# A polynomial-sketch attention and feed-forward kernel on one core: sketch loads on another queue, a new order of all steps, a last store in two halves

## The chip, the cores and the metric

The kernel runs on one core of one Trainium2 chip. The metric is the device time of one execution in microseconds, as the median of several runs. The engines are named as in the profile: PE is TensorE's matmul, PEld its loading of weights, DVE is VectorE, ACT is ScalarE, POOL is GpSimd, and SP is SyncE, whose queue issues most transfers.

## The reference

Two blocks follow each other. The first is an attention whose scores are a product of two sketches; `S1` and `S2` are 8 x 32 in float64, and q, k, v are 4 batches x 4 heads x 1088 positions x 32 in float32:

```python
def phi(x):                                   # 64 features of each position
    a = einsum('rd,bhsd->bhsr', S1, x)
    b = einsum('rd,bhsd->bhsr', S2, x)
    return einsum('bhsi,bhsj->bhsij', a, b).reshape(..., 64)
q_p, k_p = phi(q), phi(k)
kv = einsum('bhsf,bhsd->bhfd', k_p, v)        # summed over positions
z = k_p.sum(axis=2)
x = (q_p @ kv) / (q_p . z + 1e-06)            # then heads side by side: 4352 x 128
```

The second is a multiplicative feed-forward block with float64 weights, `((x @ w1) * (x @ w2)) @ w3 @ w_out`, with 128 model and 1024 inner columns. The result is 4352 x 128 in float32. The denominator can come close to zero, so the kernel splits operands into a leading part and a rest and multiplies these apart.

## The kernel before

The kernel is a set of 952 named steps. Each step is a small function that issues one or a few instructions. The text `ORDER` (lines 61 to 115) lists the names, the steps are issued in that order, and lines 1526 to 1534 chain the instructions of each engine, so that every engine works through its own steps strictly in the listed order. Nothing is reordered later: an instruction that waits holds up all that its engine has behind it. `POOL` and `ACTS` (lines 52 to 58) name the steps that run on GpSimd and ScalarE; other vector steps run on VectorE (`on`, line 148). `SLOTS` (lines 28 to 44) gives each new tile its buffer by hand; the kind `b` is the eight PSUM banks.

The names say what a step works on. `s.` is the preparation of the sketches: `s.load` loads S1 and S2 (line 252), `s.words` to `s.rest` turn float64 words into float32 parts, `s.T`, `s.R` and `s.blk` spread them over the partitions. `k0` to `k3` are the keys of the four batches. Of them `load` and `loadr` fetch the main part (8 x 128 positions a head) and the remaining 64 positions, `max`, `g`, `lead` and `rest` find a scale and split the keys (lines 566 to 596; `rest` is one subtraction on line 596), `gram0` to `gram4` multiply the split keys with themselves (line 604), `Gm` to `Nr` make the denominators' operand out of that, `kp` makes the 64 features (line 622), `kv` and `kvr` sum them with the values (lines 714 and 721). `kr0` and `kr1` handle the remaining keys of two batches at once (`kr0.kp`, line 785, on GpSimd). `q0` to `q4`, `q6` and `qr` are the queries in groups; their steps run from `tr` and `max` through products `A0`, `C0`, `C1` (lines 964 to 1298), splits `sm`, `st`, `sh`, `sl`, `sc`, the sum `al`, the products `p01`, `p2`, `p12`, the denominator `dn`, `de`, `rc`, the features `phi` and the result `x`, which `xT` copies as the operand of the feed-forward block. `w0` to `w10` load and convert the weights (the last sum on GpSimd, lines 442 and 445), and `f0` to `f7` multiply w3 by w_out (line 478).

The feed-forward block works on eight groups of 512 rows, `g0` to `g7`, and one of 256, `gr`. Each has eight chunks; `g0.3a` and `g0.3b` are the two products of chunk 3 (lines 1448 and 1458), `g0.3c` copies the first out of PSUM on ScalarE, `g0.3m` multiplies them on VectorE (line 1464), and `g0.3o` adds the product into the output (line 1471). These 128 x 512 products are the main matmuls. A group ends with `oT` and `st`, four stores on the sync queue. The last group `gr` has two row halves, with products `o0` and `o1` (line 1478), copies `oT0` (ScalarE) and `oT1` (VectorE), and stores `st0` (ScalarE's queue) and `st1` (sync queue), 64 KB each (line 1432).

72 idle matmuls on a tile of zeros (`warm0` to `warm28`, line 221, in groups of 16, 10, 6, 4, 2 and 1) are steps like the others.

In the order before, the sync queue starts with `s.load`, `k0.loadr`, `q0.load`, `k1.loadr`, `k1.load`, and ScalarE's queue with `k0.load0`, `k0.load1`. The gram of the fourth batch comes right behind the `kv` of the third on TensorE:

```python
"... kr1.kp q4.sc q4.al k2.kv0 k2.kv3 k2.kv1 k2.kv2 k3.ab k2.kvr k3.gram0 k3.gram1 k3.gram2 k3.gram3 k3.gram4 ..."
```

Of the kernel before, what the change touches and what calls it, by code (L numbers as in the profile page):

```python
# [66 lines left out]
k1.lead0 k1.tr1 warm23 q0.A0 warm15 w1.load kr0.ab warm4 warm12 kr0.abc k1.rest0 q1.l2 warm13 warm7 warm18 q0.C0 k0.N0
kr0.kp w1.m v0.load q0.sma q0.C0t q0.sta k0.N1 k0.kv0 k0.kv3 k1.gram0 k1.gram1 k0.kv1 q1.l1 k0.kv2 kr1.load v0.loadr
k0.kvr s.RC k0.Na warm10 warm21 kr1.tr k0.kvc k0.kvm q0.sha q0.sla k0.Nb k2.zero k0.Nh w0.load warm17 k1.tr0 kr1.kT
q0.sca k1.kT1 k1.kT0 k0.kzt q1.A0 k0.kz q0.A1 kr1.ab q0.al q0.phi0 q0.phi1 q1.sm q0.smy q0.sty q1.st q0.pt0 warm5  # L70
k0.kqt k0.Nl warm20 k0.Nf w0.m kr1.abc q0.pc0 q0.pt1 q0.shy q1.rm q0.C1 k1.gram2 k1.gram3 k1.gram4 q0.pc1 warm19 q0.x0
q1.load k0.Nr q0.sly q0.C1t q0.x1 w0.c q0.scy q0.p01 q0.p2 q1.sh q0.p12 q0.dn s.KS w0.j q1.C0 q0.de q1.sl q0.rc q0.xs
q0.xt q0.xT k1.ab w0.a1 v1.zero k2.load k2.loadr k2.max w1.c warm24 w0.a0 warm22 g0.3a q1.sca q1.p01 g0.3c k2.g
v1.loadr k1.Gm k2.lead0 q1.scy q1.al w2.load q1.p2 q1.p12 k1.abt q1.restT q1.dn g0.1a g0.3b w1.j q1.de k0.kq q1.rc
k1.Gt g0.3m q1.bs g0.2b w1.a0 q1.phi g0.0a g0.5a g0.4a q1.pt0 g0.0c w2.c g0.1c w3.load w2.m k2.rest0 q1.pt1 g0.6a
g0.2a q1.pc0 w2.j k1.Ga k1.kp0 q1.pc1 g0.5c g0.2c g0.6c k2.gram0 q2.tr k1.Gb k1.T0 k2.gram1 k1.T1 q2.max k1.Ta k1.Tb
k1.Ts w2.a0 w4.load q1.x w1.a1 k2.gram2 k2.gram3 k2.gram4 k1.N0 k1.N1 s.AR warm16 k2.Gm q1.xT g1.7a q2.l2 k2.Gt k2.Ga
g0.6b g0.0b w3.c q2.l1 k1.Na k1.Nb k1.Nr k2.Gb w4.m g0.4c g0.6m g0.1b g0.7a g0.0m q2.rm w4.c q2.C0 q2.A0 q2.C1 g0.1m
w4.j w3.j g1.7c warm28 g0.7c w3.m g1.4a g1.2a g0.7b q3.tr q2.Ct g0.2m g1.6a q2.At g1.6c w4.a0 w3.a0 g1.1a g1.7b
q2.load q3.max q4.tr w6.load v1.load w2.a1 w4.a1 g1.2c f1.t g0.7m w3.a1 g1.1c w6.c q3.l2 g1.5a g1.7m q3.l1 q2.sm f0.t  # L80
g1.3a g0.4b f1.m w9.load warm27 f0.m q2.st q2.sh q4.max f0.o q2.sl g1.5c g0.4m q2.sc f1.o g1.3c g1.2b q2.p01 q3.rm
v2.zero k1.kp1 q2.al q2.p2 q2.p12 g1.2m k1.kv0 k2.T0 k1.kv2 k1.kv3 k2.T1 k1.kv1 k1.kvr q3.C0 q3.A0 q3.C1 w5.load
k1.kvc g1.4c k1.kqt k2.Ta k2.Tb q2.dn k2.Ts q2.de w6.j q2.rc g1.0a q3.Ct q2.bs g1.3b g1.6b g1.5b g1.3m q2.phi0 q3.At
w6.m g0.5b w5.m w5.c g1.5m g1.1b g1.0b g1.6m q3.sm g0.0o w9.c k1.kq w9.m g0.1o g1.0c k2.N0 k2.N1 q2.pT0 g0.5m q2.x0
g1.0m q3.st g1.1m q2.restT warm11 k3.zero w6.a0 k2.Na q3.sh w7.load kh2.load w6.a1 q3.sl w9.j k2.Nr w5.j q2.xT0 g1.4b
w9.a0 w9.a1 w5.a0 f3.t g1.0o q3.load g2.6a w10.load k3.loadr g2.6b g1.1o g2.1a g2.6c q4.l2 q4.l1 w7.m g2.1c w7.c g2.6m
g1.4m k2.Nb f6.t f3.m q3.sc g2.3a g2.7a g2.7c f3.o g2.3c q3.p01 q3.al k2.kT1 w5.a1 q3.p2 q3.p12 q3.dn k2.kT0 q4.rm
f6.m f6.o w10.c w8.load k2.ab w8.c q4.C0 q4.A0 q4.C1 w7.j k2.abt warm9 g2.4a f2.t q4.Ct g1.6o g2.0a f2.m g2.2b k3.load
q4.At q4.sm q3.de w7.a0 g2.0c f2.o v2.loadr w7.a1 kh3.load g0.2o f4.t q3.rc w10.m f4.m g2.2a k2.kp0 g0.6o f4.o q3.bs
w8.m w8.j g1.3o w8.a0 v2.load q3.phi0 g2.2c g2.4c w10.j q3.pT0 q3.x0 w8.a1 g0.3o q3.xT0 g2.7b w10.a0 w10.a1 k2.kp1  # L90
f5.t k3.max q6.tr f5.m g3.0b k3.kT1 g2.7m q3.restT f7.t g3.0a f5.o g3.0c g3.0m g3.3a g0.5o g3.3c g2.1b g2.2m g3.4a
g1.4o g1.5o k3.kT0 q6.max k3.g g2.1m g3.4c g2.5b f7.m f7.o g1.2o g2.0b q4.st q4.sh k3.lead0 q4.sl g3.7a g1.7o g3.7c
k3.rest0 kr1.kp q4.sc q4.al k2.kv0 k2.kv3 k2.kv1 k2.kv2 k3.ab k2.kvr k3.gram0 k3.gram1 k3.gram2 k3.gram3 k3.gram4
k2.kvc q4.p01 k2.kqt q4.p2 g2.0m k3.abt k3.Gm g0.4o g2.5a q4.p12 g2.5c k2.kq q4.dn q4.de k3.Gt g2.5m g3.6b g2.4b g2.0o
g3.6a q4.rc g3.6c k3.Ga q4.bs g1.oT g2.4m q4.phi0 q4.phi1 q4.pT0 k3.Gb g0.7o g3.4b g3.4m v3.zero k3.kp0 v3.load
v3.loadr g3.3b g2.4o g2.3b g2.3m g3.6m q4.pT1 g0.oT qr.max g3.2a g3.1a g2.6o g2.5o g3.2b g2.3o g3.3m k3.kp1 g3.1c
g3.2c qr.l2 k3.T0 k3.T1 k3.Ta g3.2m q4.x0 q4.x1 k3.kv0 k3.kv1 k3.Tb k3.N0 k3.kv3 k3.kv2 k3.kvr k3.Ts q6.l2 q6.l1 k3.N1
q6.rm k3.Na q4.xT0 warm6 k3.Nr k3.Nb q4.xT1 g4.2a g2.2o g5.2a g4.2c q6.C0 q6.A0 k3.kvc q6.C1 g5.2c q6.At q6.Ct q6.sm
k3.kqt g2.1o g4.3a g3.0o g5.4a g4.0a g2.7o g5.3a q6.st g4.0c g5.4c g5.3c g4.3c q6.sh q6.sl g5.0a q6.sc q6.p01 q6.al
q6.p2 q6.p12 g5.3b g2.oT g5.3m q6.dn g5.4b g5.7a q6.de k3.kq q6.rc qr.l1 qr.rm q6.bs q6.phi0 q6.phi1 g5.4m g5.1a  # L100
q6.pT0 g3.1b g5.1c g3.5a g5.7b g3.5c g5.0c g5.7c g3.1m q6.pT1 g3.4o g3.5b g3.3o q6.x0 q6.x1 q6.xT1 q6.xT0 g5.1b g5.7m
g5.1m g3.5m g5.0b g6.6a g3.7b g5.0m g3.7m qr.C0 g6.6c qr.A0 qr.C1 qr.At warm25 g6.0b g6.0a g6.0c g6.0m qr.Ct qr.sm
g5.2b g7.4a g4.1a g6.5a g4.4a g4.4c g4.1c qr.st qr.sh qr.sl g3.1o g5.2m g7.2a g3.6o g3.2o g4.5a g3.5o g4.5c g7.2c
g7.0a g4.4b g5.0o g5.1o g5.5a g5.2o g7.0c g7.4c g5.5c g6.2a qr.sc g4.4m qr.al g7.6a g6.4a g6.2c g6.5c g6.4c g5.6a
qr.p01 g5.6c g7.5a g6.7a g7.6b g7.5c g5.4o g6.2b g7.6c g7.0b g5.6b g5.5b g6.7c g6.2m g4.0b g7.4b g5.3o g5.5m g5.6m
g7.5b g6.4b g7.4m g5.5o qr.p2 g7.6m g6.1a g5.6o g3.7o g4.2b qr.p12 g4.0m g7.0m g7.5m g6.7b qr.dn g4.6b g6.5b g6.7m
g3.oT g6.5m g7.2b qr.de g4.6a g4.6c g7.2m g4.6m g6.6b g5.7o g7.3a g6.3a g4.7a g6.4m g4.2m g6.6m g5.oT g7.7b g6.1b
g7.7a g7.3c g7.7c g7.7m qr.rc g7.3b qr.bs g5.st g7.1b g6.3c g7.0o g7.1a g7.1c g7.6o g6.1c g6.3b g7.5o g4.0o g4.7c
g7.4o g6.3m g7.3m g7.1m qr.phi0 g7.2o qr.pT0 qr.x0 g4.4o qr.xT0 g4.5b gr.7a gr.7c gr.1a g7.3o g6.1m gr.1c g4.5m g3.st
g0.st g7.1o g7.7o g4.1b g4.1m gr.4a gr.7b gr.1b gr.3b gr.0b gr.3a gr.4c gr.3c gr.7m g7.oT gr.3m gr.1m g4.7b gr.2a  # L110
# [1454 lines left out]
```

## Time and profile before

| | |
|---|---|
| median of 3 runs | 254.58 us (254.56 to 255.01) |
| the profiled execution | 254.37 us, its span 252.6 us |
| granted TensorE clock | 1.00 throughout |
| busy: PE, DVE, ACT, POOL | 246.1, 160.0, 99.7, 66.8 us |
| first main matmul (a_ps, line 1448) | 30.29 us |
| last matmul ends | 249.41 us |
| from HBM, to HBM | 19.40 MB, 2.23 MB |

The span runs from the first to the last instruction; the profiled execution's own time is 1.77 us longer. TensorE's matmuls are pipelined, so the starts of successive ones are what shows a pause. VectorE is busy for 0.92 to 0.98 of nearly every 6 us between 6 and 36 us, and less and less after 90 us; GpSimd is busy for 15.4 us of the first 30.3, and for 1.1 us behind 200. Transfers take place before 90 us for the most part; the stores follow after 200.

### The profile page before, as it was taken

What the parts mean: (1) busy time and instruction counts of PE and PEld (TensorE: products, weight loads), DVE (VectorE), ACT (ScalarE), POOL (GpSimd) and SP (SyncE); (2) the same over time, 40 slices, a digit from 0 to 9 for tenths busy, and PEclk for the clock granted to TensorE, in tenths of its full rate; (3) what the DMA queues carried; (4) which work ended last, traced back from release to release, by engine and by line L of the source; (5) the groups of instructions that cost most, each with busy time, mean ns of one, the idle gap of its engine ahead of it and who ended that gap; (6) DMA issues with size and microseconds to landing.
All of it is one profiled execution on the core that took longest, in us unless ns stands there. A gap on an engine that the chain in (4) does not pass through costs nothing.

```text
span 252.6 us, 5980 instructions
## 1 busy us (share of the span) xinstructions
PE 246.1 (97%) x2503; PEld 137.9 (55%) x2503; DVE 160.0 (63%) x358; ACT 99.7 (39%) x183; POOL 66.8 (26%) x99
## 2 busy tenths in 40 slices
PE   8799999999999999998999999999999999999994
PEld 6689845457456576456446444444444444456554
DVE  2999998989998995938677597550115371424040
ACT  4588398763918543340225143213340012211010
POOL 4644535393546309203540016010000001000000
PEclk9999999999999999999999999999999999999999
DMA  6867793996679930200000000000000007205014
GB/s 182 262 173 263 222 241 84 259 254 139 160 206 235 249 90 0 85 6 3 3 0 3 3 0 1 4 0 0 3 0 0 0 2 123 44 0 83 0 28 76
DMA packets 31130, 22.01 MB, mean 87 GB/s; under 512 B 21248, under 2 KB 25600, under 8 KB 30976
## 3 DMA queue, kind: packets, MB, share of 16 engines
q1 hardware_dynamic: 30416, 21.05, 33.9%
q10 hardware_dynamic: 688, 0.59, 0.7%
q8 instruction: 19, 0.31, 0.5%
q14 instruction: 7, 0.06, 0.1%
HBM read 19.40 MB, written 2.23 MB: 86 GB/s over the span
## 4 chain that ended last, share of the span: by engine, by line
PE 95%; issue 1%; DMA 1%; POOL 1%; ACT 1%; DVE 0%; SPq 0%; POOLq 0%; ACTq 0%
PE a_ps L1448 23%; PE b_ps L1458 23%; PE ps_o L1471 22%; PE ps_w3o L478 6%; PE ps_g L604 3%; PE ps_x L1408 2%; PE idle_ps L221 2%; PE ps_ac L1294 2%; PE ps_kv L714 2%; PE ps_or L1478 1%; DMA s_raw<-in_S_dram 1%; PE ps_ab L672 1%; PE ps_ab L647 1%; PE ps_xt L1195 1%; PE ps_kt L630 1%
## 5 line engine op out<-in xcount | busy, mean ns | idle before, releaser
L1464 DVE TENSOR_TENSOR ab<-ffa,b_ps 128x512 f32<-128x512 f32 (+1 forms) x72 | 44.9, 649 | 60.8 <-PE b_ps L1458 40.9
L1453 ACT COPY ffa<-a_ps 128x512 f32<-128x512 f32 (+1 forms) x72 | 38.6, 566 | 96.4 <-PE a_ps L1448 93.8
L1448 PE MATMUL a_ps<-xT,w 128*128 128x512 f32 (+1 forms) x144 | 66.7, 570 | 0.0
L1458 PE MATMUL b_ps<-xT,w 128*128 128x512 f32 (+1 forms) x144 | 65.5, 569 | 0.0
L1471 PE MATMUL ps_o<-ab,w3o 128*128 128x512 f32 x128 | 62.3, 594 | 0.0
L1448 PEld LDWEIGHTS a_ps<-xT,w 128*128 128x128 f32 x144 | 26.5, 190 | 30.0 <-issue 23.9
L1458 PEld LDWEIGHTS b_ps<-xT,w 128*128 128x128 f32 x144 | 26.9, 190 | 29.1 <-issue 25.0
L1471 PEld LDWEIGHTS ps_o<-ab,w3o 128*128 128x128 f32 x128 | 23.9, 190 | 25.5 <-issue 24.0
L442 POOL TENSOR_TENSOR w3c<-cv_c,cv_m 128x512 int32<-128x512 int32 x16 | 20.8, 1333 | 22.0 <-DVE cv_c L431 13.7
L1389 POOL TENSOR_TENSOR ph<-s_al,s_bs 128x1024 f32<-128x1024 f32 (+1 forms) x6 | 10.8, 1808 | 52.7 <-DVE s_bs L1379 52.7
L478 PEld LDWEIGHTS ps_w3o<-wo,w3T 128*128 128x128 f32 x128 | 15.4, 192 | 3.6 <-issue 3.3
L478 PE MATMUL ps_w3o<-wo,w3T 128*128 128x128 f32 x128 | 15.6, 275 | 0.0
L221 PE MATMUL idle_ps<-zeros 128*128 128x256 bf16 x72 | 13.3, 317 | 1.0 <-DVE zeros L193 1.0
L229 ACT ACTIVATE cv_c<-raw 128x1024 f32<-128x1024 f32 x11 | 12.8, 1175 | 2.1 <-DMA raw<-in_moe_w_dram 2.1
L417 ACT ACTIVATE cv_m<-raw 128x1024 int32<-128x1024 uint32 x11 | 12.8, 1178 | 0.0
L472 DVE STREAM_TRANSPOSE w3T<-w3c 128x1024 f32<-128x1024 f32 x8 | 9.8, 1230 | 3.5 <-POOL w3c L442 3.5
L604 PE MATMUL ps_g<-kk 128*32 128x64 f32 x288 | 8.2, 225 | 2.1 <-POOL kk L596 1.1
L1346 POOL TENSOR_TENSOR s_al<-s_hl 128x128 f32<-128x128 f32 (+2 forms) x3 | 2.3, 753 | 29.7 <-DVE s_hl L1341 29.7
L1419 ACT COPY xT<-ps_x 128x128 f32<-128x128 f32 (+2 forms) x20 | 4.6, 325 | 13.1 <-PE ps_x L1408 9.5
L1397 DVE STREAM_TRANSPOSE pT<-ph 128x1024 f32<-128x1024 f32 (+1 forms) x7 | 8.2, 1164 | 2.5 <-POOL ph L1389 2.4
L221 PEld LDWEIGHTS <-zeros 128*128 128x128 bf16 x72 | 7.5, 114 | 3.9 <-issue 1.0
L604 PEld LDWEIGHTS ps_g<-kk 128*32 128x32 f32 x288 | 7.0, 109 | 2.8 <-POOL kk L596 1.2
(241 smaller groups left out, 284.3 us busy)
## 6 DMA issues: line engine op xcount, KB each, us to landing
raw<-in_moe_w_dram SPq DMA_DIRECT2D x32, 256.0 KB, 7.6
qh<-in_q_dram SPq DMA_DIRECT2D x4, 544.0 KB, 3.5
out_dram<-oT SPq DMA_DIRECT2D x33, 64.0 KB, 2.0
raw<-in_moe_w_dram SPq DMA_DIRECT2D x4, 512.0 KB, 5.8
k<-in_k_dram SPq DMA_DIRECT2D x3, 512.0 KB, 5.9
v<-in_v_dram SPq DMA_DIRECT2D x2, 512.0 KB, 6.4
raw<-in_moe_w_out_dram SPq DMA_DIRECT2D x1, 1024.0 KB, 6.0
kh<-in_k_dram SPq DMA_DIRECT2D x8, 128.0 KB, 6.3
```

What stands on the lines that cost most here:

```text
L221: pe.matmul(t, zeros, bview(zeros, [[0, 2], [1, 128]]), start=True, stop=True)
L229: act.activation(dst, hi.bitcast(F32), ACT.Prelu, scale=2.0 ** -112, alpha=-2.0 ** 32)
L417: act.mul(x["m"], words(0).bitcast(U32), 2.0 ** -29)
L442: pool.tensor_tensor(d, c, m, ALU.add)
L478: pe.matmul(t["o"], w3T[ko][:, c], wo[:, c], start=c == 0, stop=c == NC - 1)
L604: pe.matmul(o[h * D:(h + 1) * D], lhs, rhs, start=start, stop=stop, skip_group_check=True)
L1389: on(nm(f"phi{u}")).tensor_mul(x, bview(s["al"][:, u * g], [[r, g], [1, r], [0, r]]), bview(s["bs"][:, u * g], [[r, g], [0, r], [1, r]]))
L1448: pe.matmul(x["a"][:, :w], w_of(0, c), xT[g][:, c0:c0 + w], start=True, stop=True)
L1453: act.copy(x["s"][:, :w], x["a"][:, :w])
L1458: pe.matmul(x["b"][:, :w], w_of(1, c), xT[g][:, c0:c0 + w], start=True, stop=True)
L1464: dve.tensor_mul(ab_sb[g, c][:, c0:c0 + w], x["s"][:, :w], x["b"][:, :w])
L1471: pe.matmul(o_ps[g], w3o[:, c], ab_sb[g, c], start=c == 0, stop=c == NC - 1)
```

## The change

S1 and S2 are issued on ScalarE's queue in place of the sync queue, and in the new order they stand between `k0.load0` and `k0.load1`. `k0.loadr` and `k1.loadr` are the first two on the sync queue. All 952 steps have a new order, and the buffers (`SLOTS`) are assigned anew. Some steps change their engine. To VectorE from GpSimd go `k0.rest0`, `k1.kp1`, `k2.kp1`, `k3.kp0`, `q0.phi1`, `q1.p2`, `q1.p12`, `q2.al`, `q2.p2`, `q4.p12`, `q6.p12`, `q6.phi0`, `q6.phi1`, `qr.p2`, `qr.phi0`, `s.Pp`, `s.blkh`, `s.rest` and `s.sum`; to GpSimd from VectorE go `k0.Nf`, `k0.Nl`, `k0.kp1`, `k2.kp0`, `k2.rest0`, `k3.kp1`, `k3.rest0`, `q0.al`, `q0.p01`, `q0.phi0`, `q0.scy`, `q1.p01`, `q2.bs`, `q3.p01`, `q3.phi0`, `q4.p01`, `q4.p2`, `q4.sc`, `q6.p01`, `q6.p2`, `qr.bs` and `qr.p01`. `k3.lead0` goes from ScalarE to VectorE. The store `gr.st1` becomes two of 16 tokens x 4 batches each, `gr.st1` on the sync queue and `gr.st2` on ScalarE's. The work and its instructions are otherwise the same.

```diff
@@ the first steps and those around k0.kvr, k3.gram and the end
-s.load k1.zero c.ident c.mask k0.zero c.zeros warm0 k0.loadr k0.load0 k0.load1 c.act s.words s.pair s.lead q0.load
-k0.max0 k0.max1 k0.g k0.lead0 warm1 k1.loadr s.low s.sum s.four k0.tr0 k0.lead1 s.rest s.T k0.kT0 k0.rest0 warm8 q0.tr
...
-gr.5o0 gr.1o0 gr.4o0 gr.0o1 g4.oT gr.6o1 gr.5o1 gr.3o0 g6.oT g4.st g6.st gr.1o1 gr.2o0 gr.7o0 gr.4o1 gr.oT0 gr.3o1
-gr.2o1 gr.7o1 gr.st0 gr.oT1 gr.st1
+k1.zero s.zero c.mask k0.zero k0.loadr c.zeros warm0 warm10 warm11 k1.loadr warm23 warm7 warm22 c.ident q0.load
+k0.load0 k0.max0 s.load k0.load1 k1.load c.act s.words s.pair s.low s.four s.lead k0.tr0 k0.max1 s.sum k0.g k0.lead0
+k0.lead1 s.rest k0.rest0 warm20 warm24 k0.tr1 warm1 s.T k0.gram0 k0.gram1 s.tc k0.rest1 s.R s.P k0.gram2 k0.gram3
...
+s.Pp q0.A0 k0.Tb k0.Ts q0.C0 k0.abc1 w1.m w1.c k0.N0 k0.N1 v0.load k0.kp1 k1.rest0 warm8 k1.tr0 q0.sma kr0.load warm14
+kr0.tr q0.sta q0.C0t q1.max kr0.kT warm4 warm27 warm15 kr0.ab kr0.abc k0.Na q0.sha q0.sla q0.sca k0.Nh kr0.kp q0.al
+kr1.load v0.loadr q1.l2 k1.kT1 q0.phi0 k0.Nb k1.gram0 k1.gram1 k0.kv0 k0.kv3 k0.kv1 k0.kv2 k0.kvr w0.load q0.phi1
...
+f3.m q6.tr q3.restT g1.2m g3.6a q6.max f3.o q6.l2 g3.6c f4.m f4.o k3.lead0 f7.t g3.1b f5.m f7.m g3.5a q6.l1 g3.1c
+k3.rest0 k2.kT1 q4.sh q4.sl g3.5c f7.o k3.kT0 g3.1m q4.sc k3.gram0 k3.gram1 k3.gram2 k3.gram3 k3.gram4 k2.ab k2.abt
...
+gr.0o0 gr.6o0 gr.5o0 gr.1o1 gr.1o0 gr.4o1 gr.3o1 gr.2o1 gr.7o1 gr.4o0 g3.st gr.3o0 gr.2o0 gr.7o0 gr.oT0 gr.oT1 g4.st
+g6.st gr.st1 gr.st2 warm25 gr.st0
...
     @step("s.load")
     def _():
         for i, x in enumerate((S1, S2)):
-            sp.dma_start(s_raw[:, i], x)
+            act.dma_start(s_raw[:, i], x)
...
-    def rest_dst(oT, u):
-        (sp if u else act).dma_start(bass.AP(tensor=out.tensor, offset=(NT - 2 + u) * DM,
-                             ap=[[NT * DM, 32], [S * DM, B], [1, DM]]), oT)
+    def rest_dst(oT, u, t0=0, n=32):
+        (sp if u and not t0 else act).dma_start(bass.AP(tensor=out.tensor, offset=(NT - 2 + u + t0 * NT) * DM,
+                             ap=[[NT * DM, n], [S * DM, B], [1, DM]]), oT[t0 * B:(t0 + n) * B])
...
-                step(f"g{g}.st{u}")(lambda u=u: dst(z[u], u))
+                if u == 0:
+                    step(f"g{g}.st0")(lambda: dst(z[0], 0))
+                else:
+                    for i in range(2):
+                        step(f"g{g}.st{1 + i}")(lambda i=i: dst(z[1], 1, 16 * i, 16))
```

The other edits replace `dve` by `on(...)` in the steps `rm`, `sc`, `p01` and `bs`, so that `POOL` can name them.

More of the change, by code (lines that the diff above doesn't have):

```diff
@@ L52 @@
 POOL = set("""
-    k0.Nh k0.rest0 k0.rest1 k1.kp1 k2.kp1 k3.kp0 q0.phi1 q1.al q1.p12 q1.p2 q2.al q2.p12 q2.p2 q2.phi0
-    q3.p2 q4.al q4.p12 q4.phi0 q4.phi1 q6.p12 q6.phi0 q6.phi1 qr.al qr.p2 qr.phi0 s.Pp s.blk s.blkh
-    s.low s.rest s.sum
+    k0.Nf k0.Nh k0.Nl k0.kp1 k0.rest1 k2.kp0 k2.rest0 k3.kp1 k3.rest0 q0.al q0.p01 q0.phi0 q0.scy q1.al
+    q1.p01 q2.bs q2.p12 q2.phi0 q3.p01 q3.p2 q3.phi0 q4.al q4.p01 q4.p2 q4.phi0 q4.phi1 q4.sc q6.p01
+    q6.p2 qr.al qr.bs qr.p01 s.blk s.low
 """.split())
-ACTS = set("k0.lead1 k1.lead0 k2.lead0 k3.lead0 s.lead".split())
+ACTS = set("k0.lead1 k1.lead0 k2.lead0 s.lead".split())
@@ L67 @@
[L67 to L110, printed above, removed]
-g6.0o gr.5a g1.st gr.2c gr.5c g4.3b gr.2b g4.7m g4.3m gr.5b g4.1o g4.2o g4.5o g4.6o gr.6b g7.st g2.st g4.3o g6.5o
@@ new lines @@
+warm16 w3.load k1.abt k2.g q2.tr g0.5a q2.max k1.Gm q1.restT w1.a1 q3.max g0.4a g0.0a g0.3a g0.7a g0.4c g0.0c g0.2a
+q1.al q1.p01 q1.p2 q1.p12 q1.dn w0.a1 g0.5b g0.3c k2.lead0 g0.5c q1.de k1.Gt s.AR q1.rc g0.3b g0.6a k1.Ga q1.bs g0.0b
+q1.phi g0.2b g0.7c g0.6c q1.pt0 k1.Gb g0.3m k2.rest0 w4.load w5.load g0.0m q1.pt1 k1.kp1 w3.c k1.T0 k1.T1 q1.pc0
+k2.gram0 k2.gram1 k2.gram2 k2.gram3 k2.gram4 k1.Ta k1.Tb k1.Ts w3.m q1.pc1 k2.Gm g0.5m k1.N0 k1.N1 k1.Na q1.x warm18
+k1.Nb q2.l2 q2.l1 g0.2c q1.xT g0.4b q2.rm k1.Nr g0.2m w3.j q2.C0 q2.A0 q2.C1 q2.Ct q2.At w5.m w5.c g1.5b g0.4m q2.sm
@@ new lines @@
+q2.st q2.sh k2.Gt k2.Ga q2.sl w2.load q2.sc q2.p01 w4.c q2.al k1.kp0 w4.j q2.p2 g1.5a g1.6a g1.3a w4.m q2.p12 g1.3c
+g1.6c g0.1a g1.0a w2.m g1.0c g1.3b g1.2a g1.0b g1.5c g0.1c g1.7a w3.a0 w3.a1 g1.3m k2.Gb q2.load v1.load g1.1a g1.7b
+q3.l2 q3.l1 g1.0m q3.rm q2.dn w2.c g1.5m w9.load q2.de w2.j g1.2c g1.1c q2.rc f0.t k1.kv0 k2.T0 k1.kv2 k1.kv3 k1.kv1
+k2.T1 k1.kvr k1.kvc q3.C0 q3.A0 q3.C1 w2.a1 q2.bs k2.Ta g1.7c k2.Tb q3.Ct q3.At g0.1b g1.4a v2.zero q2.phi0 w2.a0
+q3.sm k1.kqt g0.7b g1.6b g1.4b g0.1m g1.7m g0.6b g1.1b q2.pT0 w8.load g1.4c k1.kq g1.4m g1.6m k2.Ts g1.1m k3.zero
@@ new lines @@
+k3.loadr q2.x0 k2.N0 k2.N1 w9.c q3.st w9.j w4.a0 w9.m q2.xT0 w4.a1 q3.sh f1.t q3.sl f0.m g2.4a g2.1a w6.load q3.sc
+k3.load w5.j q4.tr q4.max q3.al q3.p01 f0.o w8.c g2.4c q3.p2 w9.a0 w9.a1 w8.m warm21 w6.c g2.1c g2.1b g2.0a q3.p12
+g0.7m g2.1m f1.m g2.2a g2.6a g2.6c g2.5b g0.6m k2.Na q4.l2 f6.t w8.j g2.0c g2.2c q3.dn f1.o q4.l1 q3.de g2.5a q3.rc
+g2.7a g2.3a g2.7c q3.bs k2.Nr q4.rm k2.Nb f6.m w5.a0 f6.o g2.5c w5.a1 g2.0b f2.t w6.m g2.0m q4.C0 q4.A0 q4.C1 f2.m
+w6.j g2.3c w10.load w7.load q3.phi0 f2.o q4.At warm13 q4.Ct q4.sm q2.restT q3.pT0 w10.c w7.c w10.m g0.0o w7.m g2.6b
@@ new lines @@
+g1.4o g2.3b k2.kp1 g3.6b g2.3m g3.2c f5.o g1.5o k2.kp0 g3.3b g3.3m g3.6m q4.de qr.max q4.rc q4.bs g2.0o g0.5o g2.4o
+g2.6o g2.5o q4.phi0 g2.7m q4.pT0 v2.load v2.loadr q4.phi1 v3.loadr v3.load g1.2o g1.7o g1.oT g3.4a kr1.kp g0.4o g3.2b
+k3.Gt g0.7o qr.l2 g3.4c q4.pT1 k3.Ga k2.kv0 k2.kv3 k2.kv1 k2.kv2 k2.kvr k3.T0 k3.Gb k3.T1 k3.ab k2.kvc k2.kqt k3.Ta
+k3.Tb k3.abt k2.kq g2.3o g3.7b g3.2m q4.x0 q4.x1 k3.Ts k3.N0 k3.N1 q4.xT1 g2.2o q4.xT0 k3.kp0 k3.Na g3.4b k3.Nb k3.Nr
+g0.oT q6.rm g3.4m k3.kp1 k3.kv0 k3.kv1 k3.kv3 k3.kv2 k3.kvr q6.C0 q6.A0 q6.C1 q6.Ct q6.At q6.sm q6.st q6.sh q6.sl
```

65 lines of the change are left out of this document (42 added, 23 removed).

## The prediction

> **What bounds the kernel now.** I read the page first: its busy line and its row of slices say that TensorE never rests.
>
> ```profile
> PE 246.1 (97%) x2503; PEld 137.9 (55%) x2503; DVE 160.0 (63%) x358; ACT 99.7 (39%) x183; POOL 66.8 (26%) x99
> PEclk9999999999999999999999999999999999999999
> ```
>
> A busy matmul row is not proof of work, so the second view is the chain that ended last. It is one TensorE chain from 9.29 us to the end; the only pieces in it that are not matmuls are these:
>
> ```profile
> 1.20 2.50 DMA s_raw<-in_S_dram
> ...
> 6.87 1.05 issue
> 7.96 1.28 POOL kk L596
> 9.29 0.99 PE ps_g L604 x41
> ...
> 117.48 0.99 issue
> ```
>
> The third view is the timeline: the start on VectorE, then the end.
>
> ```profile
> 1.53 0.73 SPq L516 DMA_DIRECT2D k<-in_k_dram  x1
> 5.63 1.41 DVE L180 TENSOR_REDUCE k_m<-k 128x1 f32<-128x576 f32 x2 [0.87 <-DMA k<-in_k_dram]
> ...
> 248.85 0.64 ACTq L1432 DMA_DIRECT2D out_dram<-oT  x1
> 249.45 0.29 DVE L1498 COPY oT<-ps_or 128x128 f32<-128x128 f32 x1 [2.85 <-PE ps_or L1478]
> 249.77 0.62 SPq L1432 DMA_DIRECT2D out_dram<-oT  x1
> ```
>
> So four stretches can change. (1) 0 to 30.29 us, where the first main matmul (g0.3a) starts. The waits of VectorE there list three items, the last of them the 0.87 us for the keys; after 5.63 VectorE never waits, so its queue paces this stretch, and TensorE fills its spare time with idle matmuls (L221). (2) 30.29 to 249.41, where TensorE streams without a pause. (3) Inside it, 1.17 us without a matmul from 117.30 to 118.47. (4) The tail, 249.41 to 252.58. The profiled execution took 254.37 us, a span of 252.6 and 1.77 around it; the median shown is 254.58, so I add 0.21 to what I work out from the trace.
>
> **The first stretch.** The same real TensorE steps stand ahead of the first main matmul in both orders, so everything is in the time at which that matmul starts.
>
> *VectorE's queue.* max0 waits for k0.loadr, issued at 1.53; the view of line 516 has 4.0 to 4.9 us to landing (median 4.1). First on its queue it is issued at about 0.74, where S1 went before, and lands near 4.85, 0.8 us earlier. ScalarE issues S1 and S2 between k0.load0 and k0.load1: two issues of 0.34 (median of line 252) put load1, and the table load behind it, 0.7 later. The table load ended at 3.02, so s.words starts near 4.05 in place of 3.79, still before max0 is over. From max0 to q0.xs VectorE took 5.63 to 28.01, 22.4 us. The new queue takes in s.pair (0.68 from start to next start), s.sum and s.rest (0.43), rest0 (0.6, from k1.rest0's 1.36 for 1152 columns), s.blkh and s.Pp (0.6), phi1 (0.6), w1.j (0.63), and gives away kp0's twin k0.kp1 (1.15), al, phi0, Nl, Nf, scy, p01 (together 1.75) and q1.sl (0.4): +0.2. VectorE alone would start the main stage 0.8 - 0.2 = 0.6 earlier, at 29.7.
>
> *TensorE's queue.* rest0 leaves GpSimd (1.28) for VectorE (0.6), so gram0 can start near 8.85 in place of 9.29. From gram0 to the first main matmul the steps and their idle matmuls sum to 20.9 us (20.99 measured before for a sum of 21.1), plus about 0.3 of waiting for rest1: 30.05.
>
> *GpSimd's chain.* This is the risk. kr0.kp now stands behind k0.Nh, which needs k0.Na. Walking VectorE's queue from 4.85 with the distances above gives the end of Na at 20.15, so kr0.kp starts at 20.4, and k0.kvr on TensorE (20.22 before) waits for it. For kr0.kp the trace has two durations:
>
> ```profile
> L785 POOL TENSOR_TENSOR kpr<-krab x2: 633/1205/1777, 17.4 to 101.9; 128x256 f32<-128x256 f32 x2
> ```
>
> The 1.777 one began at 17.45, just after VectorE's subtraction k1.rest0 (17.38 to 18.74, two SBUF inputs); the 0.633 one at 101.91 met a transpose and a product out of PSUM. So kvr is free at 21.1 to 22.2, and 9.0 us of TensorE steps lie from it to the first main matmul: 30.1 to 31.2, and 31.5 if q0.al and phi0, also on GpSimd now, are waited for. The Trainium skill (SBUF — State Buffer, section Who interferes with whom) states this as a rule: a VectorE instruction with two SBUF inputs and a GpSimd one that reads SBUF exclude each other for a whole instruction. The trace agrees (1.777 - 0.633 = 1.14 us, and 1.2 of k1.rest0 lay ahead), and the rule speaks against every product that this change moves to GpSimd.
>
> Three bounds: 29.7, 30.05, 30.1 to 31.5. I take 30.6, near the middle of the chain's own range since VectorE's steps beside it are short (0.28): **+0.3 us**, ends -0.6 and +1.2.
>
> **Idle matmuls.** 72 in both. Ahead of the first main matmul stood 62, now 66; behind it 10, now 5, since warm25 goes behind the last matmul that counts. In a running stream one takes 0.107 (0.43 for four in the chain): **-0.54**. What lies ahead is already in the 30.6.
>
> **The 1.17 us at 117.3.** No engine released it ("issue"). Instruction queue 8 moved 19 packets and 0.31 MB, 16 KB each; TensorE's 5006 recorded instructions over 19 packets are some 260 per packet. One packet, and no other transfer, moves between 115.5 and 118.6, at about 116.15. From 115.60 to 117.30 TensorE ran 299 instructions: k2.kv, k3.ab, k2.kvr and k3.gram are one run of 464 short ones. My reading: a packet's worth was used up faster than the next arrived, some 2.8 us after TensorE entered the one before (115.67 to 118.47). In the new order k2.kv stands far behind k3.gram; the run is 320 instructions (a weight load and a matmul for each pass, two passes in float32, counted from the steps), and 3072 lie ahead of it, twelve times 256. With some 25 waits counted in, a packet ends inside f7.m, 1.4 us ahead of the run, and the next is needed 232 instructions into it, 1.3 us later: 2.7 us against 2.8. So about 0.1 remains, 0.3 allowed for data traffic: **-0.9**, ends -1.17 and 0. The other runs (k2.gram, k3.kv with q6.C0) have main matmuls between, over 3.3 us per 256 instructions.
>
> **The tail.** The last products are now those of row half 0: oT0 (ScalarE, 0.27), then st2 and st0 issue on ScalarE, in this order. st2's data is ready 0.9 us earlier, so it can issue while the copy runs; its length, a half of 64 rows, lies between 0.33 (line 909's shortest) and 0.64. st0 then starts 0.45 to 0.7 after the last matmul instead of 0.36, and is still the whole 64 KB. st1 and st2 save nothing, being earlier anyway: **+0.1**, ends 0 and +0.35. Were there no st2 ahead, the copy alone would decide and the term be zero.
>
> **The middle.** VectorE's queue is lighter by 1 to 4 us over most of the stream (sums of its steps at equal TensorE work), GpSimd's heavier by up to 8 at 90 us and 5 at the end. TensorE paused nowhere there but at 117.3, so nothing is left to gain; a loss can come from any step that now ends late. **+0.2**, ends 0 and +1.5.
>
> **Sum:** 0.3 - 0.54 - 0.9 + 0.1 + 0.2 = -0.84. 254.37 - 0.84 = 253.5, with the 0.21 **253.7 us**. About 0.2% (0.5 us) is what a measurement of this kernel can tell from no change.
>
> **Rivals.**
> *GpSimd paces the first stretch fully:* first main matmul at 31.5, so +1.2 in place of +0.3: the sum is +0.06, **254.6**, the same. For it: VectorE's next step phi1 waits for GpSimd's al. Against it: long two-input products are rare there. Chance 0.17.
> *Slower, GpSimd holds k3.gram0:* k3.rest0 goes from VectorE (1.36) to GpSimd, where 640 columns took 1.55, so 1152 need 2.8; it stands behind ten products of w5 to w10 (mean 1.33, line 442). After k3.lead0 VectorE has f7.t (1.2) and TensorE f7.m and g3.5a (1.8) before the gram, 3.0 in all against 2.8. It decides from the point where TensorE is less than 2.8 us from gram0 when lead0 ends, or a two-input VectorE step goes first, as at 17.45. Price 1.4 to 2.6, at k2.gram0 likewise: on top of the other terms 253.7 + 2.0 = **255.7**. Chance 0.24.
> *The 1.17 stays:* if it is not code loading, regrouping does not remove it, the term is zero and the sum +0.06: **254.6**. For it: no row names the cause. Against it: it is the only such pause, inside the densest run. Chance 0.07. One page of the Trainium skill (Runtime: NRT & Kernel Launch, section Instruction fetch mechanics) gives TensorE a buffer of 2048 instructions, refilled 256 at a time; by that 464 short ones could not empty it, and this rival would hold. The packets agree with the 256, and the pause in a run of 464 speaks for the shorter buffer of two blocks that the same section also names.
> *Forecast:* 0.52.
>
> Faster holds the forecast, 0.52; same holds the first and third rival, 0.24; slower 0.24. All terms at their low ends give 252.3, at their high ends 256.9; leaving out a tenth at each side, 252.6 to 255.9.
>
> **What would show it.** k_m's first reduction starts near 4.85 and ps_g near 8.85; a_ps first at about 30.6; "issue" in the chain around k3.gram below 0.3; two ScalarE issues after the last ps_or, ending later than before. Wrong if TensorE shows pauses released by POOL kk or POOL kpr beyond 1 us in all, or if k0.loadr lands no earlier for being first.

## The result, and the profile after

The changed kernel takes 258.63 us (median of 4 runs, 258.6 to 259.04), the kernel before 254.8 beside it: 1.0155 times as long, 95% interval 1.0137 to 1.0172. I had predicted 253.7. The profiled execution has a span of 256.9 us against 252.6. In the experiments further down the granted clock of single executions lies between 0.976 and 1.000 and their times scatter by a few microseconds, so sizes around a microsecond are read from the profiled execution, whose clock is told where it is below 0.996.

The page of the changed kernel, its busy line and its row of clocks:

```profile
PE 246.4 (96%) x2503; PEld 138.6 (54%) x2503; DVE 167.8 (65%) x359; ACT 97.1 (38%) x181; POOL 71.2 (28%) x99
PEclk9999999999999999999999999999999999999999
```

TensorE is as busy as before (246.1), in a span that is 4.3 us longer: the loss lies where it waits. I divide the span as the prediction did. The first main matmul (a_ps) starts at 33.84 instead of 30.29, **+3.55**; from there to the last matmul's end it is 216.79 us instead of 219.12, **-2.33**; from there to the end of the span 6.26 instead of 3.17 us, **+3.08** (the parts are rounded; the last matmul of the changed kernel is the idle `warm25`, which ends 0.11 us behind the last product).

The chain that ended last begins with these pieces (start, length, what):

```profile
1.23 0.78 ACTq L252
2.05 0.29 ACTq L252
2.37 5.20 DMA k<-in_k_dram
7.58 0.75 DVE k_m L180
```

The chain of the kernel before began with S; this one reaches VectorE through the second half of the first keys, and no other piece of it outside TensorE is as long as that transfer. The timeline shows why it is late (start, duration, engine, what, and in brackets the idle time before it and what ended it):

```profile
0.74 1.42 SPq L516 DMA_DIRECT2D k<-in_k_dram  x2
...
1.23 1.10 ACTq L252 DMA_DIRECT2D s_raw<-in_S_dram  x2
...
2.20 0.61 SPq L909 DMA_DIRECT2D qh<-in_q_dram  x1
...
2.37 0.42 ACTq L504 DMA_DIRECT2D k<-in_k_dram  x1
...
4.09 0.75 DVE L180 TENSOR_REDUCE k_m<-k 128x1 f32<-128x576 f32 x1 [3.15 <-DMA k<-in_k_dram]
...
7.58 0.75 DVE L180 TENSOR_REDUCE k_m<-k 128x1 f32<-128x576 f32 x1 [1.53 <-DMA k<-in_k_dram]
```

k0.loadr, first on the sync queue now, did let the first reduction start early (4.09, 5.63 before). But k0.load1 (256 KB) went out at 2.37, just behind the queries (544 KB, 2.20), and VectorE waited for it until 7.58. The first gram matmul starts at 10.30 (9.30 before).

Ten microseconds later, in the same timeline:

```profile
17.68 1.95 POOL L622 TENSOR_TENSOR kp<-kab 128x1024 f32<-128x1024 f32 x1 [4.13 <-ACT kab L653]
17.76 1.91 DVE L850 TENSOR_TENSOR T_p<-T_p 32x32 f32<-32x32 f32 x1
...
18.16 0.25 PE L856 MATMUL ps_N<-T_p,P2a 32*32 32x16 f32 x8
19.60 1.34 DVE L596 TENSOR_TENSOR kk<-k,kk 128x1152 f32<-128x1152 f32 x1
...
19.73 0.24 PE L862 MATMUL ps_N<-T_p,P2b 32*32 32x8 f32 x8 [1.32 <-DVE T_p L850]
```

k0.Ts on VectorE, a 32 x 32 sum that took 0.17 to 0.18 us in each of its four places before (line 850), took 1.91: it ends together with the product k0.kp1, which the change put on GpSimd. Before, the view of that line is:

```profile
L850 DVE TENSOR_TENSOR T_p<-T_p x4: 170/180/181, 16.1 to 135.6; 32x32 f32<-32x32 f32 x4
```

Matmul N1 on TensorE waits for it, and so does all that VectorE has behind it. The second way is the one that reaches the first main matmul: VectorE's queue leads to q0.al and q0.phi0 on GpSimd, and TensorE waits for these once more.

```profile
23.99 0.45 POOL L1097 TENSOR_TENSOR s_al<-s_hla 128x128 f32<-128x128 f32 x1 [0.23 <-DVE RC L873]
24.52 1.57 POOL L1135 TENSOR_TENSOR ph<-s_al,s_bs 128x512 f32<-128x512 f32 x1
...
26.15 0.65 PE L1155 MATMUL ps_ph<-ident,ph 128*128 128x128 f32 x4 [0.27 <-POOL ph L1135]
```

From the end of q0.phi0 to the first main matmul it is 7.74 us here, and 7.73 to 7.75 us in all the profiled executions of this order below but that of kp_wait, where TensorE stands still for 0.62 us in between.

The pause of 1.17 us inside k3.gram is gone. The chain has that stretch in one piece with no "issue" in it:

```profile
110.18 0.86 PE a_ps L1448 x2
111.05 1.82 PE ps_g L604 x86
```

The end, first the timeline, then the waits of the sync queue (what waited, for what, total, times, longest):

```profile
245.27 8.65 SPq L1426 DMA_DIRECT2D out_dram<-oT  x6
249.66 0.29 DVE L1498 COPY oT<-ps_or 128x128 f32<-128x128 f32 x1 [1.64 <-PE ps_or L1478]
250.35 0.27 PE L221 MATMUL idle_ps<-zeros 128*128 128x256 bf16 x1
250.55 0.27 ACT L1498 COPY oT<-ps_or 128x128 f32<-128x128 f32 x1 [5.12 <-PE ps_or L1478]
250.61 1.31 ACTq L1432 DMA_DIRECT2D out_dram<-oT  x2
254.02 0.61 SPq L1432 DMA_DIRECT2D out_dram<-oT  x1
```

```profile
SPq L1426 <- DMA out_dram<-oT: 4.4, 1, 4.4
```

The ScalarE stores are out by 251.9, as I had expected. But the sync queue stands still for 4.4 us between the first and the second of g6's four stores, waiting for a transfer to finish, and gr.st1, whose data was ready at 249.95, goes out last, at 254.02. The records of the instructions say which transfer: every one counts on one of eight semaphores, given out in turn (100, 102, 104, 105, 106, 107, 108, 110), and waits for the one that last counted on the same. The stores of g3 count on 104, 105, 106 and 108, those of g4 go on with 100: 107 and 110 were given to gr.st2 and gr.st0 in between. Exactly eight further on, g6's second store (107) and fourth (110) wait for these two. gr.st2 was issued at 250.61; its transfer took 1.9 us; the second store of g6 went out at 252.52. The order of `ORDER` binds each engine's own queue only, and the turn of the semaphores follows another order.

### The profile page after: what moved, and what is told of

It is laid out like the page before. It is cut to its first block, busy times and chain, and to the rows that moved or that the text cites. A ratio compares the mean times of both kernels' runs of the same rounds, so it can differ in the third digit from the quotient of the medians.

```text
span 256.9 us, 5987 instructions
## 1 busy us (share of the span) xinstructions
PE 246.4 (96%) x2503; PEld 138.6 (54%) x2503; DVE 167.8 (65%) x359; ACT 97.1 (38%) x181; POOL 71.2 (28%) x99
## 3 DMA queue, kind: packets, MB, share of 16 engines
q1 hardware_dynamic: 30320, 21.01, 33.7%
## 4 chain that ended last, share of the span: by engine, by line
PE 87%; DVE 4%; DMA 2%; ACT 2%; POOL 1%; ACTq 1%; issue 1%; POOLq 0%
PE b_ps L1458 23%; PE a_ps L1448 23%; PE ps_o L1471 22%; PE ps_w3o L478 6%; PE ps_x L1408 2%; DMA k<-in_k_dram 2%; PE ps_ac L1294 2%; PE ps_g L604 2%; PE ps_or L1478 1%; PE ps_kv L714 1%; DVE k_m L180 1%; DVE kk L596 1%; PE ps_ab L672 1%; PE ps_xt L1195 1%; POOL ph L1135 1%
## 5 line engine op out<-in xcount | busy, mean ns | idle before, releaser
L1458 PE MATMUL b_ps<-xT,w 128*128 128x512 f32 (+1 forms) x144 | 66.6, 571 | 0.0
L1448 PE MATMUL a_ps<-xT,w 128*128 128x512 f32 (+1 forms) x144 | 64.5, 569 | 0.0
L1389 POOL TENSOR_TENSOR ph<-s_al,s_bs 128x1024 f32<-128x1024 f32 x4 | 8.8, 2204 | 11.5 <-DVE s_bs L1379 11.4
L1487 DVE STREAM_TRANSPOSE oT<-ps_o 128x512 f32<-128x512 f32 x8 | 5.7, 714 | 8.8 <-PE ps_o L1471 8.8
L596 POOL TENSOR_TENSOR kk<-k,kk 128x1152 f32<-128x1152 f32 (+1 forms) x3 | 7.6, 2531 | 12.0 <-DVE kk L177 5.6
L1379 POOL TENSOR_TENSOR s_bs<-ay_C,s_rc 128x128 f32<-128x128 f32 (+1 forms) x2 | 0.7, 352 | 35.7 <-DVE s_rc L1374 35.7
```

Source lines behind the costliest of these rows:

```text
L596: on(f"k{b}.rest{u}").tensor_sub(chunks(kk[b][:, 1], u), chunks(k_sb[b], u), chunks(kk[b][:, 0], u))
L1448: pe.matmul(x["a"][:, :w], w_of(0, c), xT[g][:, c0:c0 + w], start=True, stop=True)
L1458: pe.matmul(x["b"][:, :w], w_of(1, c), xT[g][:, c0:c0 + w], start=True, stop=True)
```

## The experiments

**The tail: semaphores or traffic?** The two ScalarE stores get a dependency on g6's last store that orders them without a wait, so that they take their semaphores after it.

```diff
+    for ins in late["gr.st2"] + late["gr.st0"]:
+        tc.add_manual_dep(ins, late["g6.st"][-1].name, behind, reason="order")
```

> The changed kernel with one thing different at the end: the two ScalarE stores (gr.st2, gr.st0) come behind the last group's stores in the program's order, with the same queues and the same order on each, so that they take their completion semaphores after g6.st instead of before it. Theory A (the second store of g6.st waits for the completion of gr.st2 because both count on one semaphore): SP issues all four stores of g6.st between 247.7 and 250, gr.st1 right after its copy at about 250.0 to 250.7; from the last matmul to the end of the span 3.2 us instead of 6.26; time 258.6 - 3.1 = 255.5 us. Rival B (the transfers at the end are slow because five groups' stores crowd there): the wait of 4.4 us in front of SP's store stays, the time stays within 0.5 us of 258.6.

Measured: span 253.9 in place of 256.9, tail 3.50 in place of 6.26; 256.85 us median (lowest 255.66), 1.0077 times the kernel before (1.0034 to 1.0119). Five of the ten executions lie between 255.66 and 255.91, near the expected 255.5, and five between 257.79 and 259.43; what parts them is not shown.

```profile
245.08 4.41 SPq L1426 DMA_DIRECT2D out_dram<-oT  x6
249.47 0.29 DVE L1498 COPY oT<-ps_or 128x128 f32<-128x128 f32 x1 [1.64 <-PE ps_or L1478]
249.79 0.61 SPq L1432 DMA_DIRECT2D out_dram<-oT  x1
```

The six stores take 4.41 us of the queue and not 8.65, and gr.st1 follows its copy at once. Same queues, same order on each, same bytes: theory A holds, and crowding is excluded. What is left over the 3.17 of before, 0.33 us, fits the second issue on ScalarE behind the last product.

**Is it the split?** The last store in one piece again, the rest as changed.

```diff
-                    for i in range(2):
-                        step(f"g{g}.st{1 + i}")(lambda i=i: dst(z[1], 1, 16 * i, 16))
+                    step(f"g{g}.st1")(lambda: dst(z[1], 1))
```

> The changed kernel with the last store whole again (gr.st1 in one, on the sync queue; gr.st2 gone), all else as changed. If the split is what made the end long: tail from the last matmul to the end 3.2 us, time 255.6. If it is the place of gr.st0 (last in the order, but ahead of g6.st's stores in the program's count of semaphores, the third of them counts on the same one): SP's third store of g6.st waits until gr.st0's transfer is over, at about 252, and two stores of g6.st and gr.st1 follow; tail 5.2 to 5.9 us, time 257.7 to 258.3.

Measured: 258.22 us (2 runs), ratio 1.0122 (1.0065 to 1.0179), tail 5.98, and the sync queue waits 4.2 us in front of a store of g6, now the third. So the split is not the cause: gr.st0, which in the new order comes after the last products, is enough to do it.

**The keys.** First s.load moved behind k0.load1 on ScalarE's queue:

```diff
-k0.load0 k0.max0 s.load k0.load1 k1.load ...
+k0.load0 k0.max0 k0.load1 s.load k1.load ...
```

> The changed kernel with s.load behind k0.load1 on ScalarE's queue instead of ahead of it. Theory A (the first keys are late because two issues stand ahead of them and the transfer of the queries then runs beside them): k0.load1 is issued at 1.24 and lands at 4.1 to 4.5 instead of 7.55; the second k_m reduction starts at 6.1 to 6.6 (behind s.pair, since S lands at about 5.5) instead of 7.59; first ps_g at 9.2 instead of 10.30; first a_ps 1.0 to 1.3 earlier than 33.84; time 257.4 us. Rival B (S, now later, paces the start: s.words, s.pair and the products s.T, s.R, s.P are late instead): ps_g and a_ps within 0.3 us of the changed kernel, time 258.5 us.

Measured: span 256.1; 258.97 us median (257.84 to 260.59, the last at a clock of 0.976), ratio 1.0152 (1.0084 to 1.022). The second reduction starts at 6.60, the gram at 9.29, both as A says, the first a_ps at 32.97: 0.87 gained in place of 1.0 to 1.3, and the time did not show it. The reduction now waits behind s.pair, since S landed only at 5.77. k0.Ts again met k0.kp1 and took 1.98. This settles that the keys were late, not why. The second run leaves the order of issue on ScalarE's queue as changed and holds the queries back:

```diff
+    for ins in late["q0.load"]:
+        tc.add_manual_dep(ins, late["k0.max0"][-1].name, wait, reason="wait")
```

> The changed kernel with the queries' transfer q0.load held back until the first k_m reduction is over (so k1.load and w1.load on the sync queue behind it are late too). k0.load1 is still third on ScalarE's queue, issued at 2.37. If the queries beside it made its transfer slow: it lands at 5.2 to 5.7 instead of 7.55, the second k_m reduction starts at 5.3 to 6.2, ps_g at 8.0 to 9.0. If being issued third is what counts, whatever runs beside it: it lands after 7, ps_g stays at 10.0 to 10.3.

Measured (one run; its clock of 0.993 comes from a stretch behind 249.8, where the last matmul is over): 255.15 us, span 253.4, although the tail keeps its 6.26.

```profile
2.37 0.41 ACTq L504 DMA_DIRECT2D k<-in_k_dram  x1
3.81 0.75 DVE L180 TENSOR_REDUCE k_m<-k 128x1 f32<-128x576 f32 x1 [2.86 <-DMA k<-in_k_dram]
...
4.59 0.37 SPq L909 DMA_DIRECT2D qh<-in_q_dram  x1
...
5.30 0.73 DVE L180 TENSOR_REDUCE k_m<-k 128x1 f32<-128x576 f32 x1
```

k0.load1 goes out at 2.37 as in the changed kernel, but there is no wait in front of the second reduction at 5.30: it landed within 2.93 us, not 5.20. It was the sync queue's traffic beside it (the queries, and behind them k1.load, which moved from 2.85 to 5.00 with them, and the first weights, from 3.79 to 5.47), not the third place in the queue. The Trainium skill (DMA: Bandwidth & Descriptors, section Queues, rings and completion order) says that a DMA engine takes turns between the queues that have work for it; the 2.93 and 5.20 us agree with that. The gram starts at 8.00, the first a_ps at 30.35, which is nearly the 30.6 that I had predicted. That is luck in part: the gram comes 0.85 us earlier than I had said, and the path runs from the held queries (VectorE waits 0.4 us for them, until 8.30) through VectorE's queue to q0.al and q0.phi0, and not through kr0.kp, for which I had priced it. And k0.Ts took 0.18, since it came 0.3 us ahead of k0.kp1.

The same part alone, on the kernel before: S1 and S2 on ScalarE's queue between k0.load0 and k0.load1, the old order otherwise.

```diff
-            sp.dma_start(s_raw[:, i], x)
+            act.dma_start(s_raw[:, i], x)
```

> The kernel before with one part of the change alone: S1 and S2 on ScalarE's queue between k0.load0 and k0.load1, all steps else in the old order. The sync queue then has k0.loadr at 0.74 and the queries at 1.5, and k0.load1 is third on ScalarE's queue at 2.37. If this part alone makes the keys late: k0.load1 lands at 7 to 8, the second k_m reduction starts at about 7.6 instead of 6.31, ps_g 1.0 to 1.5 later than 9.30, first a_ps 0.8 to 1.5 later than 30.29, time 255.5 to 256.1. If the loss needed the new order: within 0.3 us of the kernel before.

Measured: 258.01 us median (256.08 at a clock of 0.993, the other three at 0.987 or less), ratio 1.010 (1.0067 to 1.0132). In the profiled execution (0.993) the first reduction, which stands behind s.pair in the old order, starts at 6.18, the second at 7.21 after a wait for the keys, the gram at 10.32 and the first a_ps at 31.97, 1.68 later than before. Of these, 1.03 stand at the gram. The rest has another reason: the granted clock of TensorE was 0.50 from 8.62 to 12.03 in this execution, and TensorE's steps behind 10.32 were slower for it. The other three, at lower clocks still, may have had such stretches too, while 19 of the 23 executions of the kernel before had a clock of 0.998 or more; so how much of the ratio comes from the clock stays open. The move of S to ScalarE's queue does delay the gram by itself, but here more by S than by the keys: S lands late (s.words at 5.22, 3.79 before) and s.pair holds the first reduction, while the keys hold the second for 0.28 us only; the queries go out at 1.56.

**The short sum and the long product.** k0.kp1 gets a wait for k0.Ts:

```diff
+    for ins in late["k0.kp1"]:
+        tc.add_manual_dep(ins, late["k0.Ts"][-1].name, wait, reason="wait")
```

> The changed kernel with one wait more: the product k0.kp1 on GpSimd starts after the short sum k0.Ts on VectorE. Theory A (k0.Ts took 1.91 us because it and the long product on GpSimd exclude each other): k0.Ts takes 0.2 us, N1 on TensorE follows N0 without the pause of 1.49 us, first a_ps 1.2 to 1.5 us earlier than 33.84, time 257.2 us. Rival B (the exclusion only moves to the next VectorE step with two SBUF inputs, k1.rest0, and to GpSimd's product, which the sums k0.kv wait for): TensorE's pause comes back at k1.gram0 or k0.kv, a_ps within 0.4 us of 33.84, time above 258.2.

Measured: 257.95 us median, ratio 1.0107 (1.0076 to 1.0139), span 256.2.

```profile
17.80 0.18 DVE L850 TENSOR_TENSOR T_p<-T_p 32x32 f32<-32x32 f32 x1
17.91 1.34 DVE L596 TENSOR_TENSOR kk<-k,kk 128x1152 f32<-128x1152 f32 x1
18.15 2.92 POOL L622 TENSOR_TENSOR kp<-kab 128x1024 f32<-128x1024 f32 x1 [4.57 <-DVE T_p L850]
...
18.28 0.22 PE L862 MATMUL ps_N<-T_p,P2b 32*32 32x8 f32 x8
```

k0.Ts is back at 0.18 and N1 follows N0. Now the product is the one that is held: 2.92 us, of which 1.1 lie beside VectorE's k1.rest0 (to 19.25), as rival B said; but nobody waits for it, and k0.kvr starts 1.61 us earlier than in the changed kernel (22.21, 23.82). Whoever starts second waits for the other's end, both ways round. The Trainium skill has this rule (SBUF — State Buffer, section Who interferes with whom, which adds that the order of issue decides who blocks); 0.18 to 1.91 and 1.95 to 2.92 agree. q0.phi0's product on TensorE comes 1.68 us earlier (24.47, 26.15). Half of the gain was lost again at once (a_ps 33.06, 0.78 earlier), most of it by something else in this execution:

```profile
25.97 0.62 issue
```

TensorE stood still inside q0.C1, with no engine to wait for, as it had inside k3.gram before the change; I come back to it.

**All three together.** The edits of t_sem, s_behind and kp_wait in one kernel:

> All three edits at once (stores' semaphores, s.load behind k0.load1, k0.kp1 behind k0.Ts). If the three losses are independent: 3.1 + 1.2 + 1.4 = 5.7 us less than the changed kernel, 252.9 us, the first a_ps near 31.2, and so 0.6% faster than the kernel before. If one of the other queues (VectorE's work alone, about 22.5 us from its first reduction to q0.xs) holds the first stretch once one of the two is gone, the two at the start give less than their sum: a_ps 31.8 to 32.6, time 253.6 to 254.4.

Measured: 255.58 us median of ten (254.86 without three at a clock of 0.980; lowest 253.41), ratio 0.9989 (0.995 to 1.0028), the profiled execution 254.32 with a span of 252.5: the 5.7 us did not come. S landed still later (s.words starts at 6.77), s.pair held the second reduction until 7.60 and the gram until 10.30, exactly as in the changed kernel. So the edit of s.load gave nothing here, and the run shows the collision alone: equal gram, k0.Ts 0.18, a_ps at 32.17 instead of 33.84, **1.67 us**. q0.al on GpSimd starts at 22.32 instead of 23.99, by the same 1.67 earlier, and TensorE waits 0.27 us for q0.phi0 in both: the collision costs through VectorE's queue, and the wait at N1 would have been hidden behind it.

**With S back on the sync queue.** As three, but S1 and S2 on the sync queue right behind k0.loadr:

> The edits of the run called three, with s.load not behind k0.load1 but back on the sync queue, right behind k0.loadr and ahead of k1.loadr and q0.load; k0.load1 is then second on ScalarE's queue. If the start is set by whichever of S and the first keys lands last: S lands at 4.2 to 4.8, before the queries' transfer runs, s.pair ends by 5.3, the second k_m reduction starts at 4.9 to 5.5 (8.6 less 3 of the run called three would be 7.60), ps_g at 7.8 to 8.3, first a_ps at 29.9 to 30.6, time 252.0 to 252.8 us, 1% below the kernel before. If VectorE's work or the product kr0.kp bounds the stretch, ps_g comes early but a_ps stays above 31, time above 253.2.

Measured: 253.10 us median (252.47 to 256.58), ratio 0.9928 (0.9902 to 0.9955). This version is faster than the kernel before, clear of the noise, though the median is 0.3 above the range that I gave. Its profiled execution (clock 0.987) is no use for the start: the granted clock of TensorE was 0.50 from 10.98 to 17.81, idle matmuls came every 0.21 us in place of 0.107, and a_ps at 32.78 carries that. The gram was at 8.56, later than the 7.8 to 8.3 expected.

**The least set of edits.** Only the stores' semaphores (t_sem) and the held queries (q_late):

> The changed kernel with two edits: the stores' semaphores as in the run called t_sem, and the queries' transfer held back until the first k_m reduction is over as in q_late. S1 and S2 stay on ScalarE's queue and k0.kp1 has no extra wait. If the late first keys were the cause of the whole first-stretch loss (the collision of k0.Ts with k0.kp1 being only a consequence of when they meet): first a_ps near 30.35 as in q_late, tail 3.5, span 250.6, time 252.1 to 252.6 us, 0.9% below the kernel before. If the 30.35 of q_late was luck of one execution, a_ps is 31.5 or later and the time above 253.5.

Measured: 253.50 us median, 252.23 lowest, ratio 0.995 (0.9922 to 0.9977); the profiled execution has a span of 250.8, a_ps at 30.55, a tail of 3.50. The span is 0.2 above the expected 250.6 and k0.Ts took 0.18, so in this execution the loss at the start goes away with the late keys, the collision included. The median is 1.0 above the range that I gave; executions at full clock reach from 252.23 to 255.88, and why they differ stays open. The profiled one has 0.88 us of "issue" at 13.66.

The same with S also on the sync queue, behind k0.loadr (`act` back to `sp` on line 252):

> As the run called five, and S1 and S2 back on the sync queue behind k0.loadr, so that k0.load1 is second on ScalarE's queue. Without the queries beside them, the first keys and S all land by about 4.2 to 4.6; if the keys still bound the start, the second k_m reduction begins near 5.2, ps_g near 7.9 or below, time 0.1 to 0.5 us below five. If VectorE's own steps (first reduction, s.pair, second reduction) bound it by now, which they should since q_late had the second reduction right behind s.pair: equal to five within 0.3 us.

Measured: 254.05 us median, ratio 0.9957 (0.9928 to 0.9985). a_ps at 30.54 is that of five, as expected; the time is not within 0.3 of five's. The profiled span is 252.7, with a wait of 0.99 us at 40.2 for VectorE's k1.Gb that five does not have. It is the exclusion again:

```profile
37.35 2.63 POOL L596 TENSOR_TENSOR kk<-k,kk 128x1152 f32<-128x1152 f32 x1 [2.65 <-ACT kk L175]
37.67 3.40 DVE L1135 TENSOR_TENSOR ph<-s_al,s_bs 128x1024 f32<-128x1024 f32 x1
```

k2.rest0, which the change put on GpSimd, starts 0.32 us ahead of VectorE's q1.phi, and this takes 3.40 us; k1.Gb stands behind it. In five, q1.phi starts 0.31 us ahead (37.02) and takes 1.23, k2.rest0 takes 3.42, and TensorE waits for neither. A third of a microsecond decides who pays. It may be part of why executions at full clock differ; the executions without a trace can't show it.

**The pause in k3.gram.** On the kernel before, two main matmuls put into the dense run:

```diff
-... g3.7a g1.7o g3.7c k3.rest0 kr1.kp q4.sc q4.al k2.kv0 k2.kv3 k2.kv1 k2.kv2 k3.ab k2.kvr k3.gram0 ...
+... g3.7a g3.7c k3.rest0 kr1.kp q4.sc q4.al k2.kv0 k2.kv3 k2.kv1 k2.kv2 k3.ab k2.kvr g1.7o g0.4o k3.gram0 ...
```

> The kernel before with two main matmuls of the second row group's outputs (g1.7o from ahead of k2.kv, g0.4o from behind k2.kqt) put between k2.kvr and k3.gram0; the same instructions otherwise. Code loading theory (a packet of 256 instructions was used up before the next arrived): the run of 464 short instructions is cut into one of 152 and one of 320 with 1.7 us between them, the pause of 1.17 us in k3.gram is at most 0.3, the stretch from the first main matmul to the last one is 0.9 to 1.1 shorter than the 219.12 before, time 253.5 to 253.8. Rival (the pause belongs to k3.gram or its operands, whatever stands ahead): 1.17 stays, time 254.6.

Measured: 253.82 us median beside 254.93, ratio 0.9949 (0.9919 to 0.9979), and the stretch from the first main matmul to the last is 218.22 in place of 219.12. The chain:

```profile
115.09 0.25 PE ps_kv L721 x8
115.34 1.91 PE ps_o L1471 x4
117.25 1.82 PE ps_g L604 x85
```

No "issue" is left, though the same instructions run in the same gram. The pause belongs to what stands ahead of it. Five executions now show such a pause, and in each TensorE goes on a fixed time after a packet of queue 8 begins to move: 116.15 to 118.47 before, 24.10 to 26.59 in kp_wait, 11.65 to 14.13 in q_late, 12.09 to 14.54 in five, 117.75 to 120.19 in b_s_act (the same gram as before), that is 2.32 to 2.49 us. Code loading fits all of them; that it is the cause is read from these times, and no run changed the loading itself. The Trainium skill (Runtime: NRT & Kernel Launch, section Instruction fetch mechanics) calls the cost of passing such a block mostly hidden; these runs show 0.4 to 1.2 us where the instructions are short.

## Why the prediction was wrong

In microseconds against the span before:

| term of the sum | predicted | measured |
|---|---|---|
| first stretch | +0.3 | +3.55 |
| idle matmuls behind the first main one | -0.54 | -0.58 |
| the pause at 117.3 (time of k3.gram on line 604) | -0.9 | -1.20 |
| middle | +0.2 | -0.55 |
| tail | +0.1 | +3.08 |
| sum | -0.84 | +4.30 |

*Right: what the change gains.* k0.loadr lands early, by more than I had said (first reduction at 4.09, 4.85 predicted). The idle matmuls are worth their term. The pause went because its run of short instructions was broken up, and b_split shows this without the rest of the change; in both, k3.gram took 1.82 us where it had taken 3.02, so the low end of my range, -1.17, was the better value. TensorE waited for no engine in the middle of this execution, so the load moved there cost nothing; the -0.55 is the difference of the other rows, and 0.22 of it lies in k2.gram.

*Wrong: "put load1, and the table load behind it, 0.7 later".* This is the step that failed first. The two issues took 1.10 us, not twice 0.34, and k0.load1 went out 1.14 us later; but the size lies in the transfer, which I did not count as one that can be slowed. Issued behind the queries, with k1.load following, it took 5.20 us instead of at most 2.93. I had followed S up to its first reader ("still before max0 is over") and load1 only up to its issue; and S was late too, s.words starting at 5.16 and not near 4.05, which cost nothing while the keys were later still. The gram came at 10.30, not 8.85: 1.45 us.

*Wrong: where the exclusion strikes.* I named the rule, priced it on kr0.kp (0.63 or 1.78) and spread 30.1 to 31.5 over it. kr0.kp took 0.62. The price fell on k0.Ts, which has two operands in SBUF, is 0.18 us long and stands in VectorE's queue ahead of all that q0.al and q0.phi0 wait for: 1.67 us at the main matmul. I had let short steps of VectorE pass as harmless ("VectorE's steps beside it are short"). The length of the waiting step does not matter; that of the one it waits for does. 1.45 and 1.67 on top of my 30.6 make 33.7, and 33.84 was measured; that this comes out so near has the same luck in it as the 30.6. Without late keys both are gone (30.35 in q_late, 30.55 in five). My three bounds took each engine's queue by itself; the path that these runs show goes from VectorE over GpSimd's q0.al and q0.phi0 to TensorE.

*Wrong: the tail.* I summed ScalarE's issues, and that part holds: 3.50 with the semaphores in order, 0.33 over the 3.17 of before and 0.44 if it is counted from the last product, so near the upper end of my 0 to +0.35. The sentence "st1 and st2 save nothing, being earlier anyway" took for granted that stores on another queue cannot be held by ScalarE's. They share eight semaphores with them, and that was the missing term, 2.76 us (6.26 to 3.50).

*The rivals.* GpSimd did not pace the stretch through kr0.kp. The condition that I had named beside it, that q0.al and phi0 are waited for, did hold (0.27 us on TensorE, 0.29 on VectorE's phi1), with VectorE's queue and not kr0.kp setting their start. GpSimd did not hold k3.gram0 either: k3.rest0 took 2.64 us there (2.8 predicted) and ended at 108.60, the gram started at 110.97 with a main matmul right ahead of it. That the kernel came out slower is no success of that rival. The 1.17 did not stay. A slip in the range: the high ends add up to 257.1, not 256.9, since 0.21 was left out there; 258.63 is beyond both.

## What to carry to other kernels

When a transfer moves to another queue, ask of each transfer behind it not only when it is issued but what will run beside it; a big one issued 0.2 us ahead can cost more than the places lost in the queue. When a long two-operand product goes to GpSimd, look for the two-operand steps of VectorE that can meet it, short ones too, and for what waits behind them; put the product where nobody waits for whichever comes second. At the end of a kernel, count the transfers that follow a late store in the turn of the semaphores, on other queues too: here the store eight places further on waited for it.
